# The place of the maxima's transposes on TensorE, and two early hash products with a bank each

## The chip, the cores and the metric

The kernel runs on one core of one Trainium2 chip. The metric is the device time of one execution in microseconds. The kernel before was timed three times: 711.45, 712.68 and 714.77 us, a median of 712.68 us. A separate execution was recorded by the hardware profiler; all rows of the trace come from that one.

## What is computed

Three layers follow each other. The first is attention with a hash mask, for 2 batches of 8 heads, 768 positions and 64 columns. The change lies in this layer alone:

```python
q_bits = (np.einsum('bhsd,dk->bhsk', q, proj) > 0)      # 6 bits of a query, the same for a key
q_bucket = np.sum(q_bits * powers, axis=-1)
mask = q_bucket[:, :, :, None] == k_bucket[:, :, None, :]
scores = scale * np.matmul(q, k.transpose(0, 1, 3, 2))
scores = np.where(mask, scores, -1000000000.0)
scores = scores - np.max(scores, axis=-1, keepdims=True)
attn = np.exp(scores)
attn = attn / (np.sum(attn, axis=-1, keepdims=True) + 1e-09)
out = np.matmul(attn, v)
```

Its output goes through a gated layer, `(x @ w1 * (x @ w2)) @ w3 @ w_out`, and then through eight experts, of which each of the 1536 rows takes one.

## The kernel before

Two heads form a pair, and there are eight pairs. The bits of a query and a key are appended to the head's own 64 rows as more rows of the matrix product, so that a pair of positions in different buckets gets a very low score. Before the exponential can be taken, the largest score of every query must be known; it becomes two more rows of the query's matrix.

The attention runs as a list of **units**, 12 for each pair (3 query tiles times 2 heads times 2 halves of the positions), 96 in all. In the text unit i is step i of the loop at line 719, which issues, in this order, to the queues of the engines. Each engine works its own queue off in order, so the order of this loop is the order on each engine.

- `stage_1` (line 312) of unit i: two products `m` on TensorE (L317, a tile with tag `s`, two buffers), then VectorE's maximum over the 768 scores (L324, called R(i) below). After the sixth unit of a half, GpSimd (POOL) makes the rows `nm` out of the twelve maxima by four small operations (L328 to L331).
- `stage_f` (line 333): the transposes of the maxima on TensorE (L335), into a tile of tag `m`; ScalarE copies the result (L337, `rT`), and SP issues two DMAs (L340) that put the rows into the two query heads. In the kernel before this stands in the units that follow a half, 6, 12, 18 and so on up to 96. These sixteen are called f0 to f15 below, f0 in unit 6, f15 at step 96.
- `hash_half` (line 234): the products `z` with the projection for half the positions (L240, tag `m`), and VectorE's comparison that makes bits of them (L249). For the second pair (pair 1) the two halves stand in units 6 and 7. For the later pairs, two at a time, they stand in the fifth and sixth unit of every second pair.
- The preparation of the weights: `w34_step` issues products of `w3` and `w_out` (L544). Each of eight results is transposed (L519), multiplied (L527) and summed (L535) in three units on end, through `todo_at`, each with a tile of tag `m`. In the profile these stand in units 30 to 32, 38 to 40, 46 to 48, 54 to 56, 62 to 64, 70 to 72, 78 to 80 and 86 to 88.
- `stage_2` (line 345) of the position tile nine units behind: four products `s` on TensorE (L352), ScalarE's exponential (L353), the sum on POOL (L359). It needs the rows that `stage_f` sent. Its first tile of a half stands three units behind f.
- `stage_a` (line 361), two units further behind: the product with the values (L367). After each pair `stage_n` (line 376) sums the denominators (L383, tag `m`).

Tag `m` has a single buffer, one bank of PSUM: a new tile of that tag can be written when the last reader of the tile before is done with it. Tag `w` has one as well, and the weight products use it from unit 22 on.

The opening differs: pair 0's hash products go through the four banks `m`, `w`, `u` and `a` (line 711), and the last of its bits are made after the maximum of unit 5 (line 809). Unit 6 needs them.

Of the kernel before, what the change touches and what calls it, by code (L numbers as in the profile page):

```python
# [20 lines left out]
P = 128  # L21
# [27 lines left out]
HS = S // 2  # L49
# [107 lines left out]
def body(tc, qT, kT, vP, w1d, w2d, w3d, wod, mod, wgate, mbias, e1, e2, cst, out):  # L157
# [30 lines left out]
    def ps(tag, shape, name):  # L188
        return psum[0].tile(shape, F32, tag=tag, name=name, bufs=nbuf.get(tag, 1))
# [39 lines left out]
    def load_v(p):  # L229
        b, hp = divmod(p, HP)  # L230
        v_t[p] = r_v([P, QT, P])
        SP.dma_start(v_t[p], vP[b, hp])

    def hash_half(pairs, half):
        lo, hi = 64 * (pairs[0] % 2), 64 * (pairs[-1] % 2) + 64
        z = ps("m", [P, HS], f"z{pairs[0]}{half}")
        for p in pairs:
            for j, nm in enumerate("qk"):
                r = 64 * (p % 2) + 32 * j
                PE.matmul(  # L240
                    z[r:r + 32, :], cs[:, 96 + 32 * j:128 + 32 * j], raw_t[p, nm][:, half * 384:half * 384 + 384],
                    start=True, stop=True, tile_position=(0, r),
                )
        if half == 0:
            bt = r_bt([P, S], F32R)
            for p in pairs:
                bt_t[p] = bt
        bt = bt_t[pairs[0]]
        DVE.tensor_scalar(  # L249
            bt[lo:hi, half * HS:half * HS + HS], z[lo:hi, :], cs[lo:hi, 2:3], cs[lo:hi, 0:1], ALU.is_ge, ALU.mult)  # L250
# [8 lines left out]
    def brow(hd):  # L259
        return 64 - 64 * hd  # L260
# [72 lines left out]
    def stage_f(p, half):  # L333
        t = ps("m", [P, P], f"f{p}_{half}")
        PE.transpose(t[0:12, :], nm_t.pop((p, half))[:, 12:24], ident)  # L335
        rT = r_rT([12, P], F32R)
        ACT.copy(rT, t[0:12, :])  # L337
        for hd in range(2):
            r = brow(hd) + NB
            SP.dma_start(  # L340
                head_t[p, hd, "q"][r:r + 2, 0, half * HS:half * HS + HS].bitcast(F32),
                rT[6 * hd:6 * hd + 6, :].bitcast(F32),
            )
# [145 lines left out]
    def fill():  # L489
        if dq and isinstance(dq[0], int):  # L490
            dq[0:1] = piece(dq[0])
        if dq:
            dq.pop(0)()
# [224 lines left out]
    NU = len(units)  # L718
    for i in range(NU + LEAD + LAG + 2):
# [45 lines left out]
        p, ph = divmod(i, 12)  # L765
        if i < NU:
# [1 line left out]
                load_pair(p + 3)  # L768
            stage_1(units[i])
            fill()  # L770
        if ph in (0, 6) and 0 < i <= NU:
            stage_f(*divmod(i // 6 - 1, 2))
        if p == 0 and ph in (6, 7):
            hash_half([1], ph - 6)
        elif p % 2 == 1 and p + 1 < NPAIR and ph in (HASH, HASH + 1):
            hash_half([p + 1, p + 2], ph - HASH)
        for fn in todo_at.pop(i, []):
# [669 lines left out]
```

## Time and profile before

| what | value |
|---|---|
| median of three runs | 712.68 us |
| the profiled execution's own time | 713.29 us |
| its span, first to last instruction | 711.5 us |
| mean granted TensorE clock | 0.974 of full speed |
| TensorE matmul busy | 666.1 us, 94% of the span |
| VectorE, ScalarE, GpSimd busy | 382.2, 315.1, 320.6 us |
| instructions | 11037 |

The profiled execution lies 0.6 us above the median, and its span 1.8 us below its own time. A row of the timeline gives start, duration, engine, line, operation, tiles, shape and count; in brackets stands how long the engine had been idle before it and whose work ended that. Instructions of one line that follow each other are merged into one row. A row of the windows gives the busy time of PE, PEld, VectorE, ScalarE and GpSimd with the number of instructions, then the granted clock.

### The profile page before, as it was taken

What the parts mean: (1) busy time and instruction counts of PE and PEld (TensorE: products, weight loads), DVE (VectorE), ACT (ScalarE), POOL (GpSimd) and SP (SyncE); (2) the same over time, 40 slices, a digit from 0 to 9 for tenths busy, and PEclk for the clock granted to TensorE, in tenths of its full rate; (3) what the DMA queues carried; (4) which work ended last, traced back from release to release, by engine and by line L of the source; (5) the groups of instructions that cost most, each with busy time, mean ns of one, the idle gap of its engine ahead of it and who ended that gap; (6) DMA issues with size and microseconds to landing.
All of it is one profiled execution on the core that took longest, in us unless ns stands there. A gap on an engine that the chain in (4) does not pass through costs nothing. (4 is left out here: it accounts for less than half of the span.)

```text
span 711.5 us, 11037 instructions
## 1 busy us (share of the span) xinstructions
PE 666.1 (94%) x4004; PEld 506.4 (71%) x4004; DVE 382.2 (54%) x611; ACT 315.1 (44%) x534; POOL 320.6 (45%) x316
## 2 busy tenths in 40 slices
PE   5988999989998999799999999999998999999994
PEld 1444655656555655366999999898987999899983
DVE  6787675746576664857361212121175765665550
ACT  7255554535546554454341313131213765565551
POOL 8489767677767667555260505050214132011110
PEclk9599999999999999899999999999999999999998
DMA  7746545273645634230312020200017786766630
GB/s 226 238 169 171 199 136 182 78 210 103 194 140 144 198 99 128 88 120 1 107 48 60 2 59 1 60 1 30 1 53 270 269 286 232 235 207 210 209 119 5
DMA packets 42122, 94.06 MB, mean 132 GB/s; under 512 B 6784, under 2 KB 12464, under 8 KB 42064
## 3 DMA queue, kind: packets, MB, share of 16 engines
q1 hardware_dynamic: 39984, 86.76, 38.7%
q0 software_dynamic: 2080, 6.56, 2.7%
q8 instruction: 33, 0.54, 0.3%
q14 instruction: 25, 0.20, 0.1%
HBM read 72.98 MB, written 12.98 MB: 121 GB/s over the span
## 5 line engine op out<-in xcount | busy, mean ns | idle before, releaser
L618 PEld LDWEIGHTS ab<-x,w 128*128 128x128 f32 x1152 | 139.9, 191 | 10.5 <-issue 4.8
L618 PE MATMUL ab<-x,w 128*128 128x256 f32 x1152 | 144.5, 285 | 0.6 <-ACT ss L387 0.6
L324 DVE TENSOR_REDUCE nm<-m 128x1 f32<-128x768 f32 x96 | 91.1, 955 | 81.1 <-PE m L317 80.7
L359 POOL TENSOR_TENSOR acc<-acc,pt 128x770 f32<-128x770 f32 x61 | 113.4, 1860 | 31.6 <-ACT pt L353 30.7
L353 ACT ACTIVATE pt<-s 128x768 f32<-128x768 f32 x96 | 77.9, 812 | 104.8 <-PE s L352 91.7
L352 PE MATMUL s<-q,k 128*128 128x384 f32 (+1 forms) x384 | 88.1, 353 | 6.8 <-DVE nm L324 6.1
L629 POOL TENSOR_TENSOR g<-gf,g 128x256 fp32r<-128x256 f32 x48 | 35.4, 736 | 127.4 <-ACT g L628 127.2
L367 PE MATMUL a<-pt,v 128*64 128x385 f32 x384 | 86.3, 530 | 0.0
L352 PEld LDWEIGHTS s<-q,k 128*128 128x128 f32 (+1 forms) x384 | 71.1, 197 | 16.6 <-DVE nm L324 7.4
L1118 DVE TENSOR_TENSOR eu<-er,eu 128x1024 fp32r<-128x1024 f32 x56 | 67.4, 1223 | 23.0 <-ACT eu L1117 22.4
L317 PEld LDWEIGHTS m<-k,q 78*128 78x128 f32 x192 | 30.4, 198 | 64.7 <-issue 23.0
L1278 PE MATMUL e1F<-ex,eu 128*128 128x256 f32 x576 | 70.3, 284 | 0.5 <-DVE ex L1244 0.3
L1278 PEld LDWEIGHTS e1F<-ex,eu 128*128 128x128 f32 x576 | 69.7, 190 | 1.4 <-DVE ex L1244 0.5
L1304 POOL DMA_INDIRECT out<-o,sidx x13 | 13.6, 1045 | 124.7 <-ACT o L1303 119.8
L1296 PE MATMUL e2F<-eu,h 128*128 128x512 f32 x288 | 68.8, 395 | 0.0
L627 DVE TENSOR_TENSOR gf<-asb,ab 128x256 f32<-128x256 f32 x48 | 20.2, 421 | 90.4 <-ACT asb L626 90.3
L317 PE MATMUL m<-k,q 78*128 78x384 f32 x192 | 61.7, 405 | 5.7 <-DVE nm L324 2.3
L1296 PEld LDWEIGHTS e2F<-eu,h 128*128 128x128 f32 x288 | 53.4, 188 | 11.1
L1117 ACT CAST eu<-er 128x1024 fp32r<-128x1024 f32 x56 | 57.5, 1046 | 6.7 <-DMA er<-e 6.6
L544 PE MATMUL w<-wo,w 128*128 128x512 f32 x192 | 58.6, 413 | 0.8 <-POOL w L466 0.8
L914 PE MATMUL x2p<-w,g 128*128 128x512 f32 x240 | 58.1, 397 | 0.0
L359 POOL TENSOR_TENSOR acc<-pt,pt 128x770 f32<-128x770 f32 x16 | 29.6, 1851 | 52.4 <-ACT pt L353 52.4
(198 smaller groups left out, 780.6 us busy)
## 6 DMA issues: line engine op xcount, KB each, us to landing
er<-e SPq DMA_DIRECT2D x56, 512.0 KB
cr<-w3d SPq DMA_DIRECT2D x16, 512.0 KB
cr<-wod SPq DMA_DIRECT2D x8, 512.0 KB
cr<-w1d SPq DMA_DIRECT2D x8, 512.0 KB
wfd<-cT SPq DMA_DIRECT2D x16, 256.0 KB
cr<-w2d SPq DMA_DIRECT2D x8, 512.0 KB
st<-wfd SPq DMA_DIRECT2D x16, 256.0 KB
raw<-kT SPq DMA_DIRECT2D x8, 384.0 KB
```

The lines of the kernel that those rows point to most:

```text
L317: PE.matmul(s[:, half, 0:HS], q[0:KROWS[hd], 0, qt * P:qt * P + P], k[0:KROWS[hd], 0, half * HS:half * HS + HS], start=True, stop=True,)
L324: DVE.tensor_reduce(nm[:, 3 * hd + qt % 3:3 * hd + qt % 3 + 1], s[:, :, 0:HS], AX.XY, ALU.max, negate=True)
L352: PE.matmul(s[:, hd, 0:HS], k[0:n, i, c * P:c * P + P], q[0:n, i, cl], start=(i == 0), stop=(i == 1))
L353: ACT.activation(pts[j % 4][:, :, 0:HS], s[:, :, 0:HS], AF.Exp, scale=SCALE)
L359: (DVE if on_dve else POOL).tensor_add(acc, pts[(j - 1) % 4] if c == 1 else acc, pts[j % 4])
L367: PE.matmul(a_t[p, half][64 * hd:64 * hd + 64, :], v[:, c, 64 * hd:64 * hd + 64], pts[j % 4][:, hd, :], start=(c == 0), stop=(c == QT - 1) ...
L544: PE.matmul(w34p[f], w3_t[f][:, st, g, :], wo[:, mv, g, :], start=(g == 0 and k == 0), stop=(g == 7 and k == 2))
L618: PE.matmul(ab[:, j, :], w12[j][:, st, c, fs], x[:, mv, c, :], start=(c == 0 and i == 0), stop=(c == 3 and i == 2))
L914: PE.matmul(st["ps"], g_t[ch][:, a, f, i * P:i * P + P], w34[b][:, f, :], start=(f == 0 and k == 0), stop=(f == 7 and k == 2),)
L1118: DVE.tensor_sub(t[:, 1, sl], raw, t[:, 0, sl].bitcast(F32))
L1278: PE.matmul(o[f], w[:, st, c, fs], x[:, mv, c, :], start=(c == 0 and i == 0), stop=(c == 3 and i == 2))
L1296: PE.matmul(o, h[:, st, f, sl], w[:, mv, f, :], start=(f == 0 and k == 0), stop=(f == 7 and k == 2))
```

## The change

Three edits. `stage_f` keeps its place in unit 6, and all fifteen later ones stand one unit later, at steps 13, 19, 25 and so on up to 97, still behind that unit's `stage_1`. `hash_half` is cut in two, products and bits. The second pair's products go to units 1 and 2, the first half into bank `m` and the second into bank `w`; their bits stay in units 6 and 7. For the later pairs nothing changes in `hash_half`. No instruction is added or left out.

```diff
     def hash_half(pairs, half):
-        lo, hi = 64 * (pairs[0] % 2), 64 * (pairs[-1] % 2) + 64
-        z = ps("m", [P, HS], f"z{pairs[0]}{half}")
+        hash_z(pairs, half)
+        hash_bits(pairs, half)
+
+    def hash_z(pairs, half, tag="m"):
+        z = zs_t[half] = ps(tag, [P, HS], f"z{pairs[0]}{half}")
         for p in pairs:
...
+    def hash_bits(pairs, half):
+        lo, hi = 64 * (pairs[0] % 2), 64 * (pairs[-1] % 2) + 64
+        z = zs_t.pop(half)
         if half == 0:
...
-        if ph in (0, 6) and 0 < i <= NU:
-            stage_f(*divmod(i // 6 - 1, 2))
-        if p == 0 and ph in (6, 7):
-            hash_half([1], ph - 6)
+        fi = i if i <= 6 else i - 1
+        if fi % 6 == 0 and 0 < fi <= NU and (i <= 6 or fi > 6):
+            stage_f(*divmod(fi // 6 - 1, 2))
+        if p == 0 and ph in (1, 2):
+            hash_z([1], ph - 1, "mw"[ph - 1])
+        elif p == 0 and ph in (6, 7):
+            hash_bits([1], ph - 6)
         elif p % 2 == 1 and p + 1 < NPAIR and ph in (HASH, HASH + 1):
             hash_half([p + 1, p + 2], ph - HASH)
```

## Rows read from the trace of the kernel before

**Rows 1.** Windows: busy us of PE, PEld, DVE, ACT, POOL (instructions), granted clock, DMA.
```profile
36.00:67.80 31.80, 27.56 (x141) 13.85 (x139) 28.01 (x38) 18.33 (x27) 27.98 (x22) 1.00 0.53 165
67.80:145.40 77.60, 73.68 (x390) 44.45 (x386) 48.66 (x64) 42.16 (x64) 55.31 (x48) 1.00 0.51 155
...
345.00:711.50 366.50, 354.17 (x2406) 320.15 (x2404) 155.40 (x305) 136.35 (x254) 87.73 (x106) 0.99 0.35 116
```

**Rows 2.** Groups of PE lines, 25 to 360 us: count, busy, mean ns, idle before.
```profile
L335 PE MATMUL f<-ident,nm 128*12 128x128 f32 x15 | 4.2, 282 | 9.9 <-POOL nm L331 8.9 <-ACT q L269 0.8
```

**Rows 3.** The same groups for 67.8 to 267 us (f3 to f13).
```profile
L519 PE MATMUL wt<-ident,ev 128*128 128x128 f32 x28 | 4.4, 278 | 2.0 <-ACT rT L337 2.0
...
L335 PE MATMUL f<-ident,nm 128*12 128x128 f32 x11 | 3.0, 275 | 6.4 <-POOL nm L331 5.5 <-ACT q L269 0.8
...
L535 PE MATMUL pt<-ident,wT 128*128 128x128 f32 x7 | 2.1, 305 | 2.4 <-DVE bt L249 1.7 <-ACT rT L337 0.7
```

**Rows 4.** Timeline of PE in units 43 to 45 and 48.
```profile
130.13 0.62 PE L317 MATMUL m<-k,q 128*128 128x384 f32 x2
130.59 0.86 PE L544 MATMUL w<-wo,w 128*128 128x512 f32 x3
...
136.54 0.86 PE L352 MATMUL s<-q,k 78*128 78x384 f32 x4
...
145.41 0.62 PE L317 MATMUL m<-k,q 78*128 78x384 f32 x2
147.51 0.28 PE L335 MATMUL f<-ident,nm 128*12 128x128 f32 x1 [1.48 <-POOL nm L331]
148.13 0.33 PE L535 MATMUL pt<-ident,wT 128*128 128x128 f32 x1 [0.34 <-ACT rT L337]
```

**Rows 5.** Windows behind unit 48's wait and behind unit 72's.
```profile
148.40:151.80 3.40, 3.40 (x12) 2.06 (x10) 1.48 (x3) 0.74 (x1) 2.65 (x2) 0.50 1.00 263
151.80:155.20 3.40, 3.40 (x18) 2.06 (x15) 0.96 (x1) 0.81 (x2) 1.84 (x1) 1.00 0.85 254
...
228.40:231.80 3.40, 3.40 (x18) 2.29 (x16) 2.13 (x4) 1.43 (x2) 3.24 (x3) 1.00 0.92 207
```

**Rows 6.** Timeline of PE and DVE around units 90, 91 and step 96.
```profile
281.07 0.28 PE L335 MATMUL f<-ident,nm 128*12 128x128 f32 x1 [1.61 <-POOL nm L331]
...
283.81 1.01 PE L317 MATMUL m<-k,q 128*128 128x384 f32 x2
...
282.08 0.95 DVE L324 TENSOR_REDUCE nm<-m 128x1 f32<-128x768 f32 x1
...
305.31 0.28 PE L335 MATMUL f<-ident,nm 128*12 128x128 f32 x1 [0.92 <-POOL nm L331]
```

**Rows 7.** Timeline of PE and DVE in units 0 to 9, in order of time.
```profile
10.24 5.28 DVE L324 TENSOR_REDUCE nm<-m 128x1 f32<-128x768 f32 x6
...
16.37 0.98 PE L317 MATMUL m<-k,q 78*128 78x384 f32 x2 [1.91 <-ACT lo L273]
...
17.91 1.49 PE L240 MATMUL z<-raw,cs 128*32 128x384 f32 x4 [0.35 <-ACT rT L337]
...
19.48 0.69 DVE L249 TENSOR_SCALAR bt<-z,cs 64x384 fp32r<-64x384 f32 x1 [1.13 <-PE z L240]
...
22.54 1.82 DVE L324 TENSOR_REDUCE nm<-m 128x1 f32<-128x768 f32 x2
```

**Rows 8.** Timeline of SP's queue, 187 to 194 us (issues, not transfers).
```profile
187.55 1.19 SPq L389 DMA_DIRECT2D sd<-ss  x2
192.07 0.33 SPq L392 DMA_DIRECT2D sr<-sd  x1
192.49 1.41 SPq L340 DMA_DIRECT2D q<-rT  x2
```

**Rows 9.** Timeline of PE in units 60 and 63.
```profile
186.58 0.28 PE L335 MATMUL f<-ident,nm 128*12 128x128 f32 x1 [0.58 <-POOL nm L331]
...
196.41 0.86 PE L352 MATMUL s<-q,k 78*128 78x384 f32 x4
```

More of the change, by code (lines that the diff above doesn't have):

```diff
@@ L232, in load_v @@
         SP.dma_start(v_t[p], vP[b, hp])
+    zs_t = {}
     def hash_half(pairs, half):
-        lo, hi = 64 * (pairs[0] % 2), 64 * (pairs[-1] % 2) + 64
-        z = ps("m", [P, HS], f"z{pairs[0]}{half}")
+        hash_z(pairs, half)
+        hash_bits(pairs, half)
+    def hash_z(pairs, half, tag="m"):
+        z = zs_t[half] = ps(tag, [P, HS], f"z{pairs[0]}{half}")
         for p in pairs:
```

## The prediction

> **What bounds the kernel now.** I read the page's slices of the span first: TensorE (PE) is near full in almost every slice, with thinner ones in the opening and around 290 us. The windows say so by stage. From 67.8 to 145.4 us PE is busy 73.68 of 77.60 us and no other engine over 55.31, and in the long tail 354.17 of 366.50 [rows 1]. There a microsecond that PE stands still is a microsecond of the kernel, and what the attention saves is carried to the end. From 36.0 to 67.8 VectorE and POOL have 28 of 31.8 us each, PE 27.56: nobody leads there. Next the groups of PE's lines, for what PE waits for. Matmuls of the attention wait almost nowhere, but the transposes f (L335) wait 9.9 us in fifteen, nearly all of it for POOL's last small operation on the maxima [rows 2]. Between 67.8 and 267 us it is 6.4 us in eleven, and the weights' L519 and L535 wait another 2.0 and 0.7 for ScalarE's copy of f's result, since they want the same bank in the same unit; L535's other 1.7 is for the hash bits and not touched [rows 3]. Last the timeline, for one such place. In unit 48 PE issues m at 145.41, f must stand until 147.51, when POOL's operation is done, and L535 until 148.13. Unit 43, with no f, goes from m to the next product in 0.46 us [rows 4].
>
> **f3 to f13, moved behind the next unit's m.** POOL's overhang in unit 48 is 147.51 - 145.41 - 0.46 = 1.6 us. Two units and the start of a third lie between 130.13 and 136.54 [rows 4], so a unit is over 2.1 us long, and by the next unit's m POOL is done. So the waits for POOL go: 6.4. The waits behind f go where the weights' work is in the unit f leaves (30, 48, 54, 72, 78): 2.0 + 0.7. Idle is counted from the modelled end of m, 0.62 after its start, while the next product could follow after 0.46: 0.16 more at each of the seven f that waited, 1.1. And in the five places f's own 0.28 lies open, less the some 0.03 that an unhindered f takes: 1.25. Together 11.4 us.
>
> What comes in their place: in units 31, 55 and 79 f now stands ahead of L527, which writes the same bank and must wait for ScalarE's copy. Unit 48 shows the price when ScalarE is free, 0.28 + 0.34 [rows 4], so 3 x 0.62 = 1.9. L519's three waits sum to 2.0, which leaves up to 1.3 for one if the others take 0.34: 4.9 at the most. I take 1.9, since in these units ScalarE has no copy for the next pair. Net **9.6**, with 6.6 as the low end.
>
> **The clock behind unit 48.** The granted clock is 0.50 from 148.40 to 151.80, the lower level, 1.2 GHz, and PE finishes 12 records there instead of the 18 of the next stretch [rows 5]. 12 take 2.27 us at the upper level, so 1.1 to 1.7 us are lost (1.7 if all is columns); I take 1.4. It stands behind the 1.48 + 0.34 us in which PE was idle. With the waits gone I expect the clock to stay. Against it, unit 72's f waited nearly as long by the same cause, and its next stretch was granted 1.00 [rows 5], so the fall is not certain to follow such a wait, nor to stay away without one: zero is the other end. The Trainium skill (TensorE: Matmul & The Clock Gate, "What's actually happening") says that the throttled state is the default and that activity releases it. By that rule the fall goes with its idle time and the gain is the full 1.4; unit 72 neither confirms nor refutes it.
>
> **f1, f2, f14, f15.** The four have 9.9 - 6.4 = 3.5 us of idle, of which f14 has 1.61 and f15 0.92 [rows 2, 3, 6]; 1.0 is left for f1 and f2. These two lie where VectorE and POOL are as full as PE [rows 1]: between 0 and 1.0, I take 0.5. Behind f14 the next m needs the buffer that R(90) reads until 282.08 + 0.95 = 283.03, and starts at 283.81 [rows 6]: 0.7, not 1.6 (0 to 1.6). f15 stands in a stretch of PE alone: 0.9. Together **2.1**.
>
> **The opening.** In units 0 to 5 the maxima run back to back, six in 5.28 us, 0.88 each, with PE's two products of 0.62 between them [rows 4, 7]. PE has 0.26 us to spare in a unit, and a half's hash product took 1.49 us in a stretch where m took 0.98, so at a lower clock; units 1 and 2 have m's that keep up with the maxima, so there it takes less. By 1.49 x 0.62 / 0.98 = 0.9 to 1.49, less 0.26, each pushes the next maximum by 0.7 to 1.2 us, I take 1.0 [rows 7]. Their inputs are pair 1's raw rows; ScalarE reads those from unit 0 on (line 801), so I count no wait for them. So R(5), and with it the last bits of pair 0 and unit 6's m, come 2.0 later: 18.4 instead of 16.37. From there on the units are shorter. But f0 wants bank m, where the first product has lain since unit 1, and its reader, the bits' comparison, stands behind R(6) on VectorE. So m 0.62, R(6) 0.95, bits 0.69, f0 and the next m 0.9, R(7) 0.95, bits 0.69 [rows 4, 6, 7], 4.8 us and some 0.1 of handing over: R(8) starts at 23.3, where it started at 22.54 [rows 7]. **0.8 lost.** The ends hang on the clock: seven m's of 0.98 instead of 0.62, in units 6 to 12, are 2.5 us [rows 4, 7]. If the lower clock goes from there and the pushes are 0.7, a gain of 2.3; if it lasts for half of them longer and the pushes are 1.2, a loss of 2.5.
>
> **The rows sent to the heads.** On SP the moved DMAs now stand behind the two for pair p + 1's bits (line 824) or the load of v (line 783) and the weights' loads of the unit they leave, on ScalarE behind one exponential more. Two issues take 1.41 us [rows 8]. f6, moved to 130.59, would have until 136.54 [rows 4], 5.95 us: copy 0.62, issues 1.4, and the landing. The nearest row for that is L392, which waits for the two sums sent by L389, issued by 188.74: it went at 192.07 [rows 8], 3.3 us. That makes 5.4, so it fits. f9 is the tight one. SP stands at L392 until 192.07 anyway; now the load of v, an issue of about the 0.33 of L392, is ahead of f9's rows, and they are issued by 194.3. In the run before they were issued by 193.90 and used at 196.41 without idle [rows 8, 9], so they land within 2.5; 194.3 + 2.5 = 196.8 against a use at 196.41 - 0.58 - 0.16 = 195.7: 0 to 1.1 late, I take **0.5 lost**. For the others I count nothing; their cover is those two units, and without it each late half costs its lateness.
>
> **Sum.** 9.6 + 1.4 + 2.1 - 0.8 - 0.5 = 11.8 us. The profiled execution took 713.29, so 701.5; the median of the runs is 0.6 lower, 712.68, which gives **700.9 us**, 1.7% less. No instruction comes or goes.
>
> **Rivals.** POOL sets the pace of these stages: then PE meets the same backlog a little later, at a sum or an exponential, and half of the 11.0 of f3 to f13 and the clock comes back, 5.5: 706.4 us. Against it, POOL has 22 us free of 77.6, and the quiet units between two f show no idle [rows 1, 4]. Chance 0.15.
>
> The opening costs more: bank m is held from unit 1 to unit 6, f0 and all behind it wait for VectorE, and if the lower clock lasts for seven units longer, 2.5 are lost, with pushes of 1.2 another 0.4. Loss 3.7 instead of 0.8: 703.8. The Trainium skill speaks against the change here: PSUM — Partial Sum Buffer, "Summary: rules for kernel authors", asks to evacuate a bank promptly. By that rule the parked product is a cost, as by my chain; how large, the page doesn't say. Chance 0.10.
>
> The rows come too late, which ends slower: three units hid the DMAs, now two do. It decides from a landing 5.95 - 0.62 - 1.41 = 3.9 us after the last issue; beyond that each of fifteen halves waits. At 4.9 us each is 1.0 late, 15 against the 11.8 gained: 715.9 us. For it, f9's queue; against it, 3.3 us as the slowest landing in the rows [rows 8]. Chance 0.05.
>
> The moved transposes wait as long as before, because POOL is later still: 712.7. Against it, the overhang of 1.6 us in a unit of over 2.1. Chance 0.03.
>
> **How the numbers follow.** The forecast has 0.67. Its own ends: everything good adds 0.3 for the clock, 1.4 for the four f, 3.1 for the opening and 0.5 for f9, 5.3: 695.6; everything bad takes 3.0 for L527, 1.4 for the clock, 1.2 for the four f, 1.7 for the opening and 0.6 for f9, 7.9: 708.8. Not all fall to one side at once. The range of 8 in 10 takes in the first two rivals: 696.5 to 707.5. About 0.5%, 3.6 us, is what a measurement of this kernel can tell from no change. Faster than 709.1: 0.88; within: 0.07, the bad end and the rival without effect; slower: 0.05.
>
> **What would show it.** L335 waits under 1 us in all, L519 none for rT; L527 waits three times, 0.3 to 0.5 each. Quiet units keep their length. f0 waits for VectorE's bits, and R(8) starts near 23.3. The first s of a half has no new idle, but for f9's. Stretches at 0.50 behind unit 48 are gone. It is wrong if idle before L352 grows by over 2 us, or if PE's busy share of 67.8 to 263 us doesn't rise.

## The result, and the profile after

| what | before | after |
|---|---|---|
| median | 712.46 us (4 runs, 711.45 to 714.77) | 706.52 us (4 runs, 705.30 to 707.06) |
| ratio | | 0.9907, 95% interval 0.9887 to 0.9927 |
| the profiled execution's own time | 713.29 us | 707.06 us |
| its span | 711.5 us | 705.3 us |

The change makes the kernel 0.9% faster, 5.9 us. The forecast was 700.9, 11.8 us less. The sign and the main mechanism came out, but half of the gain went missing, and 706.52 lies at the slow end of the stated range of 696.5 to 707.5. The profiled execution is the slowest of its four, 0.5 us above the median.

In the kernel after, the lines have moved: m is L326, the maximum L333, POOL's last operation L340, f L344, `rT` L346, the rows' DMAs L349, s L361, the exponential L362, the weights' L519, L527 and L535 are L528, L536 and L544.

First the windows, by the stages of [rows 1], with the same columns.

```profile
36.00:67.80 31.80, 27.28 (x136) 13.45 (x136) 28.09 (x39) 18.91 (x29) 29.03 (x23) 1.00 0.55 168
67.80:145.40 77.60, 76.35 (x401) 46.53 (x402) 51.38 (x69) 44.50 (x67) 58.41 (x53) 1.00 0.55 169
145.40:263.20 117.80, 113.41 (x580) 69.17 (x580) 75.56 (x103) 61.91 (x95) 82.32 (x69) 0.99 0.51 152
```

From 67.8 to 145.4 us PE is busy 76.35 of 77.60 instead of 73.68. From 145.4 to 263.2 there are still 4.4 us of idle. The groups of PE, 25 to 360 us, say what they wait for [rows 2].

```profile
L361 PE MATMUL s<-q,k 128*128 128x384 f32 (+1 forms) x382 | 88.2, 354 | 10.5 <-DVE nm L333 7.4 <-DMA q<-rT 2.5 <-ACT pt L362 0.5
L326 PE MATMUL m<-k,q 78*128 78x384 f32 (+1 forms) x172 | 55.1, 402 | 3.5 <-DVE nm L333 2.6 <-ACT pt L362 0.8
L627 PE MATMUL ab<-x,w 128*128 128x256 f32 x341 | 44.6, 287 | 1.5 <-ACT rT L346 0.9 <-ACT ss L396 0.6
L344 PE MATMUL f<-ident,nm 128*12 128x128 f32 x15 | 4.1, 271 | 0.0
L536 PE MATMUL pg<-wT,wgs 128*32 128x128 f32 x64 | 3.4, 285 | 1.3 <-ACT rT L346 1.3
```

The transposes (L344) wait for nothing, where they waited 9.9 us. L536 now waits 1.3 for `rT`. New is that s waits 2.5 us for the rows themselves ("DMA q<-rT"), and that L627, the first early product of the gated layer, waits 0.9 for `rT`. In the same window of before, s stood 6.0 us in all:

```profile
L352 PE MATMUL s<-q,k 78*128 78x384 f32 (+1 forms) x380 | 87.2, 353 | 6.0 <-DVE nm L324 5.4 <-ACT pt L353 0.6
```

So the idle time before s grew by 4.5 us. The prediction had called it a sign of being wrong if it grew by over 2; it did, 2.5 of it for the rows and 2.0 for VectorE's maxima. PE's busy share, the other sign, rose as forecast.

To see where the time went I subtracted the start of each unit's m in the trace of before from its start after.

| m of unit | 24 | 48 | 49 | 51 | 53 | 63 | 64 | 73 | 85 | 91 | 92 | 95 | end of span |
|---|---|---|---|---|---|---|---|---|---|---|---|---|---|
| after less before, us | -0.09 | -3.31 | -6.90 | -6.79 | -3.22 | -4.11 | -2.91 | -4.94 | -6.07 | -8.66 | -4.98 | -5.60 | -6.2 |

The opening costs nothing by unit 24. Each f then gives its share: f7's place, unit 48, 3.59 alone. But between units 51 and 53 the same 3.58 is gone again, between 63 and 64 another 1.20, and between 75 and 76, not in the table, 0.22. Without these three steps the stretch from unit 24 to 85 would have gained 10.98 us; it gained 5.98. Here is the largest step in the timeline of PE:

```profile
145.68 0.27 PE L344 MATMUL f<-ident,nm 128*12 128x128 f32 x1
145.71 1.17 PE L553 MATMUL w<-wo,w 128*128 128x512 f32 x4
...
154.19 0.94 PE L361 MATMUL s<-q,k 78*128 78x384 f32 x4 [1.82 <-DMA q<-rT]
...
157.82 1.48 PE L361 MATMUL s<-q,k 78*128 78x384 f32 x4
```

f7 waits for nothing in unit 49, but the first s of its half stands 1.82 us for the rows. SP's queue in the same stretch (issues, not transfers):

```profile
143.34 0.97 SPq L448 DMA_DIRECT2D cr<-w3d  x1
144.41 2.84 SPq L398 DMA_DIRECT2D sd<-ss  x2
147.34 0.34 SPq L232 DMA_DIRECT2D v<-vP  x1
148.09 0.33 SPq L489 DMA_DIRECT2D wfd<-cT  x1
148.47 0.42 SPq L448 DMA_DIRECT2D cr<-w1d  x1
148.99 1.46 SPq L349 DMA_DIRECT2D q<-rT  x2
```

`rT` was ready at 146.24 by the trace. SP was at the sums until 147.25, then at the load of v, a store and a load of weights, all of the unit that f left, and issued the rows only at 148.99. They were then 154.19 - 150.45 = 3.7 us on their way, behind those transfers. Behind the wait, the granted clock fell, as the windows show:

```profile
152.60:156.00 3.40, 1.81 (x9) 0.99 (x10) 0.31 (x1) 0.86 (x3) 2.21 (x2) 1.00 0.50 172
156.00:159.40 3.40, 3.40 (x11) 2.67 (x13) 0.96 (x1) 0.76 (x3) 0.00 (x0) 0.51 0.01 4
159.40:162.80 3.40, 3.40 (x17) 1.86 (x18) 0.96 (x1) 3.32 (x5) 2.37 (x4) 0.99 0.00 0
```

0.51 is the lower level, 1.2 GHz; 11 records of PE instead of 17 fit in, and four products s took 1.48 us instead of 0.86. So wait and clock give back f7's whole gain in this execution. The steps behind f9 (0.70 of wait) and f11 have no such fall.

### The profile page after: what moved, and what is told of

Read it like the earlier page. It is cut to its first block, busy times and chain, and to the rows that moved or that the text cites. A ratio compares the mean times of both kernels' runs of the same rounds, so it can differ in the third digit from the quotient of the medians.

```text
span 705.3 us, 11043 instructions
## 1 busy us (share of the span) xinstructions
PE 663.0 (94%) x4004; PEld 505.9 (72%) x4004; DVE 383.4 (54%) x611; ACT 314.8 (45%) x534; POOL 319.6 (45%) x316
## 5 line engine op out<-in xcount | busy, mean ns | idle before, releaser
L627 PEld LDWEIGHTS ab<-x,w 128*128 128x128 f32 x1152 | 139.9, 191 | 11.5 <-issue 4.4
L627 PE MATMUL ab<-x,w 128*128 128x256 f32 x1152 | 144.5, 285 | 1.5 <-ACT rT L346 0.9
L333 DVE TENSOR_REDUCE nm<-m 128x1 f32<-128x768 f32 x96 | 91.4, 955 | 77.8 <-PE m L326 77.3
L368 POOL TENSOR_TENSOR acc<-acc,pt 128x770 f32<-128x770 f32 x61 | 113.1, 1853 | 26.6 <-ACT pt L362 25.1
L362 ACT ACTIVATE pt<-s 128x768 f32<-128x768 f32 x96 | 77.9, 811 | 97.5 <-PE s L361 87.9
L361 PE MATMUL s<-q,k 128*128 128x384 f32 (+1 forms) x384 | 89.0, 355 | 11.2 <-DVE nm L333 8.1
L361 PEld LDWEIGHTS s<-q,k 128*128 128x128 f32 (+1 forms) x384 | 71.0, 198 | 23.8 <-DVE nm L333 9.6
L326 PEld LDWEIGHTS m<-k,q 78*128 78x128 f32 x192 | 30.9, 200 | 63.4 <-issue 20.5
L326 PE MATMUL m<-k,q 78*128 78x384 f32 x192 | 62.0, 408 | 6.6 <-DVE nm L333 3.7
L368 POOL TENSOR_TENSOR acc<-pt,pt 128x770 f32<-128x770 f32 x16 | 29.6, 1852 | 51.1 <-ACT pt L362 51.1
```

What stands on the lines that cost most here:

```text
L326: PE.matmul(s[:, half, 0:HS], q[0:KROWS[hd], 0, qt * P:qt * P + P], k[0:KROWS[hd], 0, half * HS:half * HS + HS], start=True, stop=True,)
L333: DVE.tensor_reduce(nm[:, 3 * hd + qt % 3:3 * hd + qt % 3 + 1], s[:, :, 0:HS], AX.XY, ALU.max, negate=True)
L361: PE.matmul(s[:, hd, 0:HS], k[0:n, i, c * P:c * P + P], q[0:n, i, cl], start=(i == 0), stop=(i == 1))
L362: ACT.activation(pts[j % 4][:, :, 0:HS], s[:, :, 0:HS], AF.Exp, scale=SCALE)
L368: (DVE if on_dve else POOL).tensor_add(acc, pts[(j - 1) % 4] if c == 1 else acc, pts[j % 4])
L627: PE.matmul(ab[:, j, :], w12[j][:, st, c, fs], x[:, mv, c, :], start=(c == 0 and i == 0), stop=(c == 3 and i == 2))
```

## The experiments

All unit starts below are against the one profile of before. Each run's stretches stand here together; the text refers to them by the run's number. Negative is earlier.

| run, edit | to unit 24 | 24 to 85 | 85 to 95 | span | median | ratio, 95% interval |
|---|---|---|---|---|---|---|
| after | -0.09 | -5.98 | +0.47 | 705.3 | 706.52 | 0.9907 (0.9887 to 0.9927) |
| 1, transposes alone | -0.97 | -10.33 | +1.74 | 702.1 | 704.17 | 0.9886 (0.9854 to 0.9917) |
| 2, hash products in u, w | -1.63 | -9.51 | +1.20 | 701.5 | 704.33 | 0.9890 (0.9859 to 0.9922) |
| 3, rows first | +0.74 | -11.27 | +1.20 | 702.0 | 703.28 | 0.9864 (0.9831 to 0.9898) |
| 4, rows from ScalarE | +3.97 | -10.93 | +1.99 | 706.5 | 708.00 | 0.9925 (0.9897 to 0.9953) |
| 5, after again | +0.31 | -8.97 | +1.74 | 705.8 | 704.71 | 0.9887 (0.9864 to 0.9911) |
| 6, rows first, u, w | +0.79 | -11.27 | +1.19 | 702.0 | 702.26 | 0.9848 (0.9824 to 0.9872) |
| 7, as 6, early products w, u | -0.94 | -11.25 | -1.76 | 698.7 | 700.26 | 0.9820 (0.9794 to 0.9846) |
| 8, hash products alone | +1.01 | -1.54 | +1.15 | 710.8 | 712.87 | 1.0002 (0.9987 to 1.0016) |
| 9, after, early products w, u | +0.03 | -9.65 | +0.42 | 701.8 | 704.30 | 0.9883 (0.9860 to 0.9906) |
| 10, as 7, hash as before | -1.89 | -11.27 | -1.76 | 696.2 | 699.23 | 0.9796 (0.9777 to 0.9815) |
| 11, 7 again | -1.05 | -11.26 | -1.75 | 696.4 | 700.50 | 0.9830 (0.9803 to 0.9857) |

The kernel before took 711.89 us beside runs 1 to 4, 713.44 beside 5 to 8 and 713.49 beside 9 to 11.

### Run 1: the transposes alone

```diff
-        if p == 0 and ph in (1, 2):
-            hash_z([1], ph - 1, "mw"[ph - 1])
-        elif p == 0 and ph in (6, 7):
-            hash_bits([1], ph - 6)
+        if p == 0 and ph in (6, 7):
+            hash_half([1], ph - 6)
```

> The transposes one unit later, the second pair's hash products back in units 6 and 7, with bank m as before. My theory: units 14 to 23 are paced by VectorE and POOL and swallow whatever the opening gains or loses, so unit 24 begins at 67.7 as in the changed kernel, within 0.3 us, and the time is that of the changed kernel, 706.5, within 1 us. The rival, that the opening's work is carried to the end: unit 24 begins 0.8 or more earlier or later, and the time moves by as much.

704.17 us: the whole gain of the change, and no less, is there without the other edit. My theory missed: the time lies 2.35 us under 706.5, and unit 24 began at 66.83, not within 0.3 of 67.7. f0 waits for nothing. In its profile the groups of PE, 25 to 360 us, are

```profile
L361 PE MATMUL s<-q,k 128*128 128x384 f32 (+1 forms) x384 | 87.6, 351 | 7.9 <-DVE nm L333 6.6 <-ACT pt L362 0.9 <-DMA q<-rT 0.3
L344 PE MATMUL f<-ident,nm 128*12 128x128 f32 x15 | 4.1, 271 | 0.0
```

The rows were late by 0.3 us here, not 2.5, although SP's order around f7 is that of the kernel after. By the trace SP issued f7's rows 0.7 us behind `rT` here, 2.75 after, and s had 0.5 us to spare.

### Run 2: the early hash products in banks that nothing waits for

```diff
-            hash_z([1], ph - 1, "mw"[ph - 1])
+            hash_z([1], ph - 1, "uw"[ph - 1])
```

> The changed kernel with the second pair's hash products in banks u and w, so that f0 need not wait until VectorE has read bank m. Both theories: f0's wait of 1.84 us for the bits is gone and unit 7 begins up to 1.7 earlier, near 18.4. My theory: unit 24 begins at 67.7 all the same, within 0.3 us, and the time stays at 706.5 within 1 us. The rival: the 1.7 us are carried on, unit 24 begins near 66.0 and the time is near 704.8.

704.33 us. PE's timeline of the opening, first the kernel after, then run 2:

```profile
17.11 0.98 PE L326 MATMUL m<-k,q 78*128 78x384 f32 x2 [1.91 <-DVE q L716]
19.93 0.37 PE L344 MATMUL f<-ident,nm 128*12 128x128 f32 x1 [1.84 <-DVE bt L258]
```

```profile
17.58 0.59 PE L326 MATMUL m<-k,q 78*128 78x384 f32 x2 [1.91 <-DVE q L716]
18.03 0.28 PE L344 MATMUL f<-ident,nm 128*12 128x128 f32 x1
...
23.21 1.62 PE L361 MATMUL s<-q,k 78*128 78x384 f32 x4 [1.27 <-DMA q<-rT]
```

The product parked in bank m makes f0 wait 1.84 us for VectorE's bits; in another bank the wait is gone and f0 stands 1.9 us earlier. The first s gets 0.6 of it (23.21 against 23.80 after), since now f0's rows are late. That what the opening gains is swallowed before unit 24, as I had held, is not borne out: unit 24 came 1.5 us earlier than after. The rival's numbers, 66.0 and 704.8, came out, at 66.16 and 704.33. They don't show that the 1.7 us were carried on, since the runs without any edit there, after and 5, differ by 0.4 and runs 3 and 9 by 0.7 from each other, and run 1 has as good a time without the early products; see the opening, below.

### Run 3: the rows ahead of the unit's other transfers

SP's `flush` of waiting loads and the weights' store of the unit that f left go behind f's rows; the load of v moves one unit on.

```diff
...
+        hold[0] = i % 6 == 0 and 12 <= i < SWITCH - 1
...
             stage_f(*divmod(fi // 6 - 1, 2))
+            flush()
...
-            if j % 12 == 3 and j // 12 + 1 < NPAIR:
+            if j % 12 == 4 and j // 12 + 1 < NPAIR:
...
-        flush()
+        if not hold[0]:
+            flush()
```

> The changed kernel with the loads and stores that SP issued in the unit that f left (the values' load, the weights' loads and stores) behind f's rows again, as they were before the change. My theory, that the rows come late because they stand behind those transfers in SP's queue: the 1.82 us that the first s of f7's half waits for its rows and the 0.70 of f9's are gone or under 0.3 each, the clock's fall behind unit 52 goes too, unit 84 begins 4 us or more earlier than the 258.2 of the changed kernel, and the time is near 702. The rival, that the transfers of this stretch simply fill the 16 engines, whatever their order: f7's wait stays over 1 us and the time within 1 us of 706.5.

703.28 us, where 702 was expected, and no s waits for rows any more in the window below. SP's queue at f7:

```profile
145.18 1.10 SPq L398 DMA_DIRECT2D sd<-ss  x2
147.08 1.40 SPq L349 DMA_DIRECT2D q<-rT  x2
148.58 0.34 SPq L490 DMA_DIRECT2D wfd<-cT  x1
148.98 0.48 SPq L448 DMA_DIRECT2D cr<-w1d  x1
149.51 0.44 SPq L232 DMA_DIRECT2D v<-vP  x1
```

and its groups of PE, 25 to 360 us:

```profile
L361 PE MATMUL s<-q,k 128*128 128x384 f32 (+1 forms) x382 | 89.1, 357 | 7.0 <-DVE nm L333 6.5 <-ACT pt L362 0.5
```

The same transfers run in the same stretch, only behind the rows. From the completions in the trace I worked out how far behind the last issue the rows landed, and how long before the first s could have started (negative: s waits, or its second head does):

| | f3 | f5 | f7 | f9 | f11 | f13 |
|---|---|---|---|---|---|---|
| after, landing / to spare, us | 3.5 / 0.2 | 1.7 / 3.9 | 3.8 / -1.9 | 2.0 / -1.2 | 4.1 / -0.05 | 1.7 / 1.9 |
| run 3 | 2.8 / 1.5 | 1.1 / 4.5 | 1.5 / 3.05 | 1.1 / 1.2 | 1.2 / 3.1 | 1.1 / 2.5 |

These are the halves with a load of v in the unit that f left; the others, f4 to f12, land after 1.06 to 1.3 us in both kernels. Were the DMA engines simply full, the order would have changed nothing. From unit 24 to 85 all four kernels with this edit (3, 6, 7, 10, and 11 as the repeat of 7) gain 11.25 to 11.27 us; the kernel after gained 5.98 and in its repeat 8.97. For this stretch the cause of the missing gain is shown, and in the profile of after it is most of what is missing. The medians say less: 1.4 to 3.2 us, worked out below, and the intervals of run 3's ratio and of the two of the kernel after overlap. The Trainium skill (DMA: Bandwidth & Descriptors, "Queues, rings and completion order") says that each DMA engine takes the descriptors of one queue in their order; the trace agrees, 3.8 us behind the other transfers and 1.5 ahead of them.

### Run 4: the rows from ScalarE's queue

```diff
-            SP.dma_start(
+            ACT.dma_start(
                 head_t[p, hd, "q"][r:r + 2, 0, half * HS:half * HS + HS].bitcast(F32),
```

> The changed kernel with f's rows sent by ScalarE's own DMA queue, right behind its copy, instead of SP's. My theory: both waits of s for the rows are gone, near 702 us, if the issues on ScalarE, some 1.3 us for each half, are covered; they cost at most 0.5 us each in the 15 halves where exponentials are behind them, 7 in all, if they are not. The rival, that the engines are full: f7's s still waits over 1 us, and the time is at or over 706.5.

708.0 us, slower than the kernel after. From unit 24 to 85 it repairs what run 3 repairs (-10.93), but the opening lost 4 us:

```profile
25.91 0.66 PE L361 MATMUL s<-q,k 78*128 78x384 f32 x1 [3.06 <-DMA q<-rT]
```

f0's rows were 3.06 us late in ScalarE's queue, and from 25 to 360 us s waits 3.7 us in all for the exponential (0.5 after). The issues now stand between ScalarE's exponentials. The opening also has two more stretches at the lower clock, from 41.7 and from 62.1 us, and no run tells their part in the 4 us from that of the late rows. The runs of this kernel span 703.50 to 709.11, more than others. So the other queue is no cure.

### Run 5: the kernel after once more

No edit.

> The changed kernel once more, on the chip of the runs it is compared with. If f7's rows come late because of their place behind other transfers, with no slack left, then how late they are differs from execution to execution: this profile may show f7's s waiting 0 or 2 us, f9's 0.3 to 1.3, and the time lies between 704 and 707. The rival, that the lateness is fixed by the order of the program: f7's s waits 1.8 us again, and the time is 706.5.

704.71 us. f7's s waits 0.59, f9's 0.56, f11's 0.13: the same order and places, other sizes, and the clock did not fall behind f7. How late the rows are differs by execution; the kernel after has no slack for it. Its time differs too: this measurement lies 8.7 us under the kernel before beside it (713.44), the first one 5.9. The intervals of the two ratios overlap, and what is missing of the forecast 11.8 is 3 to 6 us.

### Runs 6 and 7: both repairs, then the early products' banks

Run 6 is run 3 with run 2's edit. Run 7 adds

```diff
-                moe_half(0, h // 2, h % 2, "wm"[h // 2 % 2])
+                moe_half(0, h // 2, h % 2, "wu"[h // 2 % 2])
```

> Rows ahead of the transfers, as in the third run, and the hash products in banks u and w, as in the second. My theory, that the two gains add up: no s waits for rows, unit 24 begins at 66.2 to 66.9 instead of 68.5, and the time is 1 to 2 us under the third run's 703.3, near 701.8. The rival, that what the opening gains is lost to VectorE and POOL before unit 24: 703.3.

> The sixth kernel, with the first products of the gated layer, which use banks w and m in turn, in w and u. They stand in the step to which f15 has moved, and in the changed kernel the first of them waits 0.9 us for ScalarE's copy of f15, since both want bank m. My theory: this wait goes and 1.0 us is gained, near 700.8. The rival, that the copy is late because ScalarE is, and the same time is lost at the rows of f15 or at the next product: no gain.

702.26 and 700.26 us. Run 6 shows the rows repaired (-11.27) but not the opening: unit 24 came at 68.58 (+0.79), where my theory had 66.2 to 66.9. So the time, 0.5 from the forecast 701.8, came out for another reason than I gave. The lower clock lasted 20.5 us in this opening; see the opening, below. Run 7 took away L627's wait. From unit 85 on it also came 3 us earlier than run 6 at unit 94, which the bank can't explain, since the first of these products is issued behind that unit's m; see run 9.

### Run 8: the hash products alone

```diff
-        fi = i if i <= 6 else i - 1
-        if fi % 6 == 0 and 0 < fi <= NU and (i <= 6 or fi > 6):
-            stage_f(*divmod(fi // 6 - 1, 2))
+        if ph in (0, 6) and 0 < i <= NU:
+            stage_f(*divmod(i // 6 - 1, 2))
```

> Only the second pair's hash products in units 1 and 2, all transposes where they were. By my chain the opening loses: f0 waits 1.8 us for VectorE's bits, unit 10 begins 0.8 later than before, and unless the clock differs unit 24 too; the time is 0 to 1 us over the kernel before. The rival, that the hash products' place is what gained: 1 to 2 us under it.

712.87 us, ratio 1.0002: alone the second edit has no effect that can be told from none; its interval allows 0.9 us of gain to 1.1 of loss. The transposes wait as in the kernel before. But this run says something on the clock. f7 stands as long as in [rows 4], for the same operation, and the clock does not fall:

```profile
148.53 0.28 PE L344 MATMUL f<-ident,nm 128*12 128x128 f32 x1 [1.48 <-POOL nm L340]
149.16 0.33 PE L544 MATMUL pt<-ident,wT 128*128 128x128 f32 x1 [0.34 <-ACT rT L346]
```

```profile
148.80:152.20 3.40, 3.06 (x16) 2.06 (x16) 1.48 (x3) 1.07 (x2) 3.29 (x2) 1.00 1.05 267
```

Between the m of units 48 and 49 this run is 1.53 us quicker than the kernel before, and at no other place from unit 24 to 85: this is what the fall at 148.4 us had cost [rows 5].

### Runs 9 to 11: what else the best version needs

Run 9 is the kernel after with run 7's bank edit alone; run 10 is run 7 with run 1's edit; run 11 is run 7 unchanged.

> The changed kernel with one edit: the early products of the gated layer alternate between banks w and u instead of w and m. Theory (what f15 and the last half lost came from bank m, which f15 or the denominators hold): the 0.9 us that the first early product waited for ScalarE's copy of f15 is gone, unit 94 starts earlier against unit 90 than in the changed kernel, and the time is 1 to 3 us under the changed kernel's, near 702 to 704 where that one has 704.7 to 706.5. Rival (VectorE sets the end of the attention, whatever bank the products have): the wait goes, but the next m or s waits as much longer, and the time is that of the changed kernel within 0.7 us.

> The best version so far (rows ahead of the other transfers in SP's queue, early products in banks w and u) with the second pair's hash products back in units 6 and 7, as in the kernel before. Theory (the transposes' place is the whole gain and the hash products' place gives nothing that lasts): the same time as the version with the products in units 1 and 2 run beside it, within 1.0 us either way. Rival (the products' move, with a bank each that nothing waits for, carries 1 to 2 us from the opening to the end): this kernel is 1 to 2 us slower than the one beside it.

> The best version so far once more, for the comparison with the other two of this call: rows ahead of the other transfers, second pair's hash products in units 1 and 2 through banks u and w, early products in banks w and u. It took 700.3 us the first time. Theory: 699.5 to 701.5, 1.5 to 1.9% under the kernel before, with no transposes waiting for POOL. Rival (700.3 was an execution with a lucky clock): 702 to 703, like the version with the early products in w and m.

Run 9: 704.30 us. The wait for `rT` is gone from L627's group, 25 to 360 us:

```profile
L627 PE MATMUL ab<-x,w 128*128 128x256 f32 x376 | 48.8, 286 | 0.6 <-ACT ss L396 0.6
```

From unit 95 to the first s of f15's half it is 0.64 us quicker than after, the 0.9 less a new 0.18 for the rows; too little to show in the median, which lies 0.4 under run 5's. Unit 94 came only 0.1 earlier against unit 90 than after, so that part of the theory fell, and the time is the rival's. What makes unit 94 early in runs 7, 10 and 11 is VectorE's order in time against POOL, below. It is read from the traces; no run sets it by itself. These three are also the only ones with both the rows first and run 7's banks, and each of the two alone (runs 3 and 9) did not have it.

Run 10 took 699.23 us and run 11 700.50. The hash products in units 1 and 2 show no gain that lasts, even with free banks: run 10 without them is the fastest kernel of all, 2.0% under the kernel before. The intervals of the two overlap, so it is not shown to be faster than run 11. Run 11's six executions spread from 698.2 to 704.1, run 10's five lie within 2.1 us.

## Why the prediction was right and wrong

**f3 to f13, with the clock: right.** The sum had 9.6 + 1.4 = 11.0 us; the runs with the rows on time gain 11.26, and 1.53 of that is the clock (run 8), so 9.7 is left where 9.6 was forecast. In the profile of after the steps outside the three late halves sum to 10.98. The three collisions with L527 were put at 0.62 each, 1.9 in all; the unit starts show 0.51, 0.78 and 0.51, 1.8. The bound of 4.9 was needless.

**The clock behind unit 48: right in size, by luck in part.** 1.4 forecast, 1.53 measured. But run 8 has the same 1.48 + 0.34 us of idle without the fall, and unit 72 in [rows 5] had said so already. In all eleven profiles with the transposes moved PE runs at full clock there; the kernel after got a fall at 156 us instead, behind its late rows. So a fall can follow such an idle time, and need not; that before had it, and run 8 not, is no effect of the change.

The Trainium skill (TensorE: Matmul & The Clock Gate, "What's actually happening") has the throttled state as the default, released by activity. By that rule the fall was to go with its idle time, and it went; that run 8 kept the clock with the same idle time the rule alone would not have told.

**The rows sent to the heads: the step that failed.** The sum had 0.5 lost, at f9 alone, and "for the others I count nothing". In the profile of after late rows cost 5.0 us, 3.6 of them at f7; in run 5, 2.3 (11.26 less 8.97). By the medians, putting the rows first brings 1.4 (run 3 against run 5) to 3.2 us (against after), measurements beside which the kernel before took 711.89 to 713.44. The working named the load of v and the weights' loads as work ahead of the rows, and then priced only f6's two issues and one landing of 3.3 us. It left out, first, the issues ahead on SP: for f7 the rows began 2.75 us after `rT`, not at once. Second, the landing, taken as 3.3 from the way of the sums in [rows 8], was up to 4.1 us behind the loads. For f7 that is 0.56 + 2.75 + 1.46 + 3.74 = 8.5 us, where two units give 6.7 (145.68 to 152.37, when PE was ready for s). f9, which I called the tight one, waited 0.70, and its step lost 1.20 by the unit starts (63 to 64), just over the 0 to 1.1 that I had given it.

The rival "rows too late" had this mechanism. It took all fifteen halves to be late by 1.0; three were, f7, f9 and f11, all with v's load ahead of their rows. So the sum stayed on the fast side.

**f14: nothing, forecast 0.7.** From unit 85 to 95 0.5 us were lost. The m behind it did come earlier (unit 91, -8.66), and unit 92 gave it back (-4.98). The s of unit 91 waits 2.83 us for the maximum R(90). Rows of PE, VectorE and POOL in the timeline of after, and then of before:

```profile
275.15 0.62 PE L326 MATMUL m<-k,q 128*128 128x384 f32 x2 [0.16 <-ACT pt L362]
...
278.71 1.49 PE L361 MATMUL s<-q,k 78*128 78x384 f32 x4 [2.83 <-DVE nm L333]
...
288.75 1.33 PE L361 MATMUL s<-q,k 78*128 78x384 f32 x4 [3.92 <-DVE nm L333]
...
275.78 2.01 DVE L592 TENSOR_TENSOR xT<-xT,nw 128x256 f32<-128x256 f32 x1 [0.79 <-POOL xT L591]
277.71 0.94 DVE L333 TENSOR_REDUCE nm<-m 128x1 f32<-128x768 f32 x1
...
284.62 2.02 DVE L596 TENSOR_TENSOR x<-xT,x 128x256 fp32r<-128x256 f32 x1
...
289.21 0.42 DVE L596 TENSOR_TENSOR x<-xT,x 128x256 fp32r<-128x256 f32 x1
...
275.71 1.80 POOL L368 TENSOR_TENSOR acc<-acc,pt 128x770 f32<-128x770 f32 x1
...
284.30 2.07 POOL L368 TENSOR_TENSOR acc<-acc,pt 128x770 f32<-128x770 f32 x1
```

```profile
281.74 0.42 DVE L583 TENSOR_TENSOR xT<-xT,nw 128x256 f32<-128x256 f32 x1 [0.79 <-POOL xT L582]
...
283.39 1.82 POOL L359 TENSOR_TENSOR acc<-acc,pt 128x770 f32<-128x770 f32 x1 [1.68 <-ACT pt L353]
...
287.95 0.97 PE L352 MATMUL s<-q,k 78*128 78x384 f32 x4 [0.74 <-DVE nm L324]
...
294.36 0.99 PE L352 MATMUL s<-q,k 78*128 78x384 f32 x4 [3.86 <-DVE nm L324]
```

With f14 out of unit 90, its s and the exponential come earlier, and so does POOL's sum (L368). It now runs while VectorE has the operation that stands ahead of R(90) (L592, L583 before): 2.01 us instead of 0.42. All eleven profiles with f14 moved have this operation at 2.01 to 2.02 and the wait at 2.83 to 2.84; the two without, before and run 8, have 0.42 and 0.74 or less. The later wait of 3.92 is not new: it was 3.86 before. So a shorter wait of PE for POOL became a longer one for VectorE. The forecast had R(90) hold up the next m. But m of unit 91 went at 275.15, ahead of R(90) at 277.71, and it is the s behind m that waits; and what POOL and VectorE do beside each other there was not looked at.

**f15: nothing, forecast 0.9.** f15 gives 1.0, and the step after it loses 1.1:

```profile
301.94 0.27 PE L344 MATMUL f<-ident,nm 128*12 128x128 f32 x1
...
304.65 1.57 PE L627 MATMUL ab<-x,w 128*128 128x256 f32 x11 [0.91 <-ACT rT L346]
```

The first early product in bank m now stands in f15's step and waits for `rT`. I had looked for collisions in bank m among the weights' products only; this is the same kind, missed (run 9).

**The opening: mechanism right, size off.** f0 waits for VectorE's bits, as forecast. R(8) came at 22.78 us, not 23.3 (before: 22.54). The pushes of the early products were smaller: unit 6's m came at 17.11, not 18.4. Unit 24 stood at -0.09, where the terms for the opening, f1 and f2 gave 0.3 lost, and run 8, with this edit alone, at +1.01. I had written that the ends hang on the clock, and the profiles fit that: unit 24 comes later the more time the opening spends at the lower clock (a granted 0.5). Run 4 with its late rows apart, it is 6.8 us in run 10 (-1.89), 10.2 in runs 1 and 2 (-0.97, -1.63), some 17 in before (0), after and runs 5, 7, 9 and 11 (-1.05 to +0.31), and 20.5 in runs 3, 6 and 8 (+0.74 to +1.01). This time differs between openings of the same program (run 6 against 7 and 11), so the term can't be read from one profile, and f1 and f2 can't be told from it. Among those with 17 us the products in banks w and u stand at -0.94 and -1.05, those with bank m at -0.09 to +0.31. Whether such a microsecond reaches the end is open: no two medians tell it from nothing.

The Trainium skill (PSUM — Partial Sum Buffer, "Summary: rules for kernel authors") asks in general for prompt evacuation, since the space is tight, and the trace agrees that parking costs: 1.84 us of f0's wait with the parked product, 0.00 with another bank (run 2).

**The tail** was not in the sum: 0.75 us, where the profile of before has one more stretch at 0.51 of the clock, from 544.3 us. It belongs to the execution and not to the change: from unit 95 to the end the other profiles lie between 1.3 us under before and 1.2 over it. With that, what went missing in this profile adds up: 4.5 for late rows, 1.2 for f14, 1.0 for f15, less 0.4 for the opening and 0.75 for the tail is 5.6, the difference between 11.8 and the 6.2 by which the spans differ.

POOL as the pace-maker did not come: no quiet unit grew, and PE is busy 116.21 of 117.80 us from 145.4 us on once the rows are on time, in run 10:

```profile
67.80:145.40 77.60, 76.35 (x402) 46.62 (x402) 51.49 (x68) 43.45 (x66) 58.53 (x49) 1.00 0.56 169
145.40:263.20 117.80, 116.21 (x613) 70.92 (x613) 76.79 (x105) 64.85 (x98) 86.33 (x71) 1.00 0.53 159
```

## What to carry to other kernels

When a step is moved later to spare one engine a wait, write down for each DMA that it issues what now stands ahead of it in its queue, issues and bytes both, and take the landing from a row with such transfers ahead. A small transfer on which the path depends should be issued before the unit's bulk loads: from unit 24 to 85 that cost nothing here and brought back 2.3 and 5.3 us against the two profiles of the kernel after. When a shorter wait starts another engine's work earlier, look at what that work will then run beside. For a tile with one buffer, list every user in the step it moves to, not only the kind that collided before.

## What the runs showed of the hardware

**A small DMA behind large ones in one queue.** f7's rows landed 1.5 us after their last issue with v, a store and a 0.5 MB load behind them, 3.8 us with the same three ahead of them in SP's queue. ScalarE's queue was no way round it: there f0's rows were 3.06 us late (run 4).

**VectorE beside POOL.** The same operation of VectorE (L596, 128x256) took 0.42 us alone and 2.02 us while POOL's sum of 2.07 us ran beside it, and L592 of after 2.01 where it took 0.42 before (rows above). In run 11 it came earlier against POOL's sum, took 0.85 us, and s waited 0.50 us for the maximum instead of 3.92:

```profile
277.49 0.85 DVE L601 TENSOR_TENSOR x<-xT,x 128x256 fp32r<-128x256 f32 x1
...
283.86 0.97 PE L361 MATMUL s<-q,k 78*128 78x384 f32 x4 [0.50 <-DVE nm L333]
```

The Trainium skill (Trainium Architecture — The Big Picture, "What this means for kernel authors") says that of the engines only these two contend for SBUF, by a shared port pair that one of them locks. The rows agree that they hold each other up, 2.02 us against 0.42; the lock itself no row shows.

So by these rows some 3 us near the end of the attention hang on when VectorE's operations meet POOL's sums. In runs 7, 10 and 11 this s waited 0.50 to 1.26 us, in all the others 2.2 to 3.9; what sets it stays open.
